# Windowed attention with routed experts on one core: later loads issued in paced pairs behind GpSimd copies, and a new mix of warm-up matmuls

## Chip, cores and metric

The kernel runs on one core of one Trainium2 chip. The metric is the device time of one execution in microseconds. Three executions were timed, and the profile is one further execution.

## What is computed

The reference is an attention with a window of 64 positions over 8 batches, 8 heads, 576 positions and 64 channels, in float32, followed by a mixture of 8 experts with equal capacity.

```python
scores = scale * np.matmul(q, k.transpose(0, 1, 3, 2))
mask = (rel >= 0) & (rel < 64)            # rel = pos[:, None] - pos[None, :]
attn = softmax(np.where(mask, scores, -1e9))
x = np.matmul(attn, v).transpose(0, 2, 1, 3).reshape(4608, 512)
logits = x @ w_gate                        # 8 experts, 576 tokens each
# tokens are given to experts in the order of all logits, best first
out[mask_e] = np.maximum(x[mask_e] @ w1[e], 0) @ w2[e]
```

## The kernel before, in words

The attention is a loop over periods m = 0 to 36 (`for m in range(M + 1)`). A batch has nine blocks of 64 queries, and a period computes two blocks, so a batch lasts four and a half periods. All engines run their instructions in the order in which the loop writes them; there is no reordering, and an engine that waits holds all that stands behind it in its queue.

In period m the loop writes, in this order: the scores of period m in two halves g = 0 and 1 (`qk`: TensorE products of line 128, then on VectorE eight reductions of line 136, four for each half, that add the mask and leave the row extreme in the tile `mx`); the gate products of a new batch (`gate_mm`, line 85, and `gate_cp`); one period after them the gate's turn (`gate_tr`, `gate_out`), which ends with the copies of `even` on GpSimd (lines 114 and 115, two for each of four pairs of blocks, eight in all); the product with the values for period m - 2 (`pv`, line 178); the exponentials of line 141 and the copies of line 153 on ScalarE; then `norm` for period m - 2 on VectorE (`r` in lines 222 and 223, the gate sums, the scaled rows). Into `norm` are woven constants (`more`, two a period, some of them iotas on GpSimd) and a list of small routing steps (`late`, two a period, some of them four comparisons of line 609 on GpSimd). At the end of the period come the stores of finished rows (`store`) and, in the periods named by `loads`, the loads of a later batch (`load_all`), all on the queue of SyncE. For batch 3 and later the gate's turn falls in periods 14, 19, 23, 28 and 32; for batches 1 and 2 the last three pairs of blocks are turned in periods 7 and 12, six copies each.

The tiles of the loop come from the pool `wk`, which gives each name three buffers in turn. `mx` is taken twice a period, once for each half:

```python
wk = ctx.enter_context(tc.tile_pool(name="wk", bufs=3))
mx = wk.tile([128, 4], FT, name="mx")
r = wk.tile([128, 2, 4], FT, name="r")
```

The first line of work in the kernel is a run of matmuls on a tile of zeros (`WARM`, line 49), before the first queries and keys have landed.

After the attention come the routing and the experts (lines 438 to 1377), which the change leaves alone.

Of the kernel before, what the change touches and what calls it, by code (L numbers as in the profile page):

```python
# [20 lines left out]
B, H, S, D = 8, 8, 576, 64  # L21
NB = S // 64
HP = H // 2
E = 8
WARM = 30
VW = 73
DM = H * D
HOLD = 14
LOADED = 9 * (B - 3) + 12


def attention(ctx, tc, c, q, k, v, vt, gate, xs, L, choices, setup, counters, mean, rows, guess):

    nc = tc.nc
# [7 lines left out]
    x = ps.tile([128, 512], FT, name="Tp", bufs=2)  # L42
    SP = [ps.tile([128, 2, 4, 128], FT, name=f"Sp{r}", bufs=1) for r in range(2)]

    z = c["zero"]
    nc.vector.memset(z, 0.0)

    for _ in range(WARM):
        nc.tensor.matmul(x[:, 0:128], z, z, start=True, stop=True)
    masks(tc, c)  # L50
    Q, K, VO, VE, VT = {}, {}, {}, {}, {}

# [35 lines left out]
    def gate_cp(b, i0, i1):  # L88
        nc.scalar.activation(VS[b][:, 64 * i0:64 * i1], VS[b, i0][:, :64 * (i1 - i0)], AF.Copy)
# [27 lines left out]
    def qk(m, g):  # L117

        Sp = [SP[g][:, r] for r in range(2)]
        bi = [divmod(2 * m + a, NB) for a in range(2)]  # L120
        for pp in range(2):
            p = 2 * g + pp
            for a, (b, i) in enumerate(bi):

                k0 = i - 1 if i else 0
                for r in range(2):
                    d = slice(64 * r, 64 * r + 64)
                    nc.tensor.matmul(Sp[r][64 * a:64 * a + 64, pp], Q[b][d, i, p],  # L128
                                     K[b][d, k0:k0 + 2, p], start=True, stop=True)
        kinds = [int(i > 0) for b, i in bi]  # L130
        mk = c["mask"][tuple(kinds)]
        st = wk.tile([128, 4, 128], FT, name="st", bufs=2)
        mx = wk.tile([128, 4], FT, name="mx")
        for h in range(4):

            nc.vector.tensor_tensor_reduce(st[:, h, :], Sp[h % 2][:, h // 2], mk, scale=-0.125, scalar=3.0e38,  # L136
                                           op0=OP.add, op1=OP.min, accum_out=mx[:, h:h + 1])
        pe = wk.tile([128, 4, 128], FT, name="pe", bufs=4)

        def exp(h):  # L140
            nc.scalar.activation(pe[:, h, :], st[:, h, :], AF.Exp, bias=mx[:, h:h + 1], scale=-1.0)  # L141

        return pe, [lambda h=h: exp(h) for h in range(4)]
# [42 lines left out]
    def norm(m, Op):  # L186

        r = wk.tile([128, 2, 4], FT, name="r")
        x = wk.tile([128, H, D], FT, name="x", bufs=HOLD + 4)
        if m % 4 == 0:  # L190
            XL[0] = wk.tile([128, 4, H, E], FT, name="l", bufs=2)
        l = XL[0]

        def scaled():
            for h in range(H):
                nc.scalar.activation(x[:, h], Op[:, h // 4, h % 4, 0:64], AF.Copy, scale=r[:, h // 4, h % 4:h % 4 + 1])
            stores.append((m, x))

        def gates():
            nc.vector.tensor_tensor(l[:, m % 4].rearrange("p (g h) e -> p g h e", g=2), Op[:, :, :, 64:72],  # L200
                                    r[:, :, :, None].to_broadcast([128, 2, 4, E]), OP.mult)
            totals()

        def totals():
            if m in ends:
                j0 = ends[m]
                if m < 32:
                    a = wk.tile([128, 4, 4, E], FT, name="a", bufs=1)
                    nc.gpsimd.tensor_tensor(a, l[:, :, 0:4], l[:, :, 4:8], OP.add)
                    nc.gpsimd.tensor_tensor(a[:, :, 0:2], a[:, :, 0:2], a[:, :, 2:4], OP.add)  # L210
                    nc.gpsimd.tensor_tensor(L[:, j0:m + 1, :], a[:, :, 0], a[:, :, 1], OP.add)
                else:
                    nc.vector.tensor_reduce(L[:, j0:m + 1, :], l[:, j0 % 4:m % 4 + 1].rearrange("p i h e -> p i e h"),
                                            axis=AX.X, op=OP.add)
                late.extend(choices(j0, m + 1))

        def values():
            nc.vector.tensor_tensor(x.rearrange("p (g h) d -> p g h d", g=2), Op[:, :, :, 0:64],
                                    r[:, :, :, None].to_broadcast([128, 2, 4, 64]), OP.mult)
            stores.append((m, x))  # L220

        return [lambda: nc.vector.tensor_scalar(r, Op[:, :, :, 72], 1e-9, None, op0=OP.add),
                lambda: nc.vector.reciprocal(r, r), gates, scaled if m > 32 else values]
# [31 lines left out]
    def load_all(b, part):  # L255
        if not part:
            Q[b] = ld.tile([128, NB, HP, 64], FT, name="Q", bufs=3)
            K[b] = ld.tile([128, NB, HP, 64], FT, name="K", bufs=3)
        else:
            VT[b] = ld.tile([128, NB, HP, 64], FT, name="VT")  # L260
            VO[b] = ld.tile([128, 5, H, VW], FT, name="VO", bufs=3)
        for t, x in ((VT[b], vt), (VO[b][:, 0:4], v)) if part else ((Q[b], q), (K[b], k)):
            t = t.rearrange("p i h w -> p (i h w)").rearrange("p (n x) -> p n x", n=4)
            n = 512 * t.shape[2]
            rows = x[b].rearrange("p x -> (p x)")[0:n].rearrange("(n p x) -> n p x", n=4, p=128)
            for i in range(4):
                nc.sync.dma_start(t[:, i], rows[i])
        if part:
            nc.sync.dma_start(VO[b][0:64, 4].rearrange("p h w -> p (h w)"),
                              v[b].rearrange("p x -> (p x)")[n:n + 64 * H * VW].rearrange("(p x) -> p x", p=64))  # L270

    M = B * NB // 2
    products, turns, loads = {}, {}, {}
# [17 lines left out]
    for m in range(M + 1):  # L291
        exps = [[], []]
        more = [lambda: next(setup, None)] * (0 if not m else 6 if m < 5 else 2)
        if m < M:
            P[m], exps = zip(*[qk(m, g) for g in range(2)])

        for x in products.get(m, []):
            gate_mm(*x)
        old = [x for x in turns.get(m, []) if x not in products.get(m, [])]
        for x in old:  # L300
            gate_tr(*x)
        for x in old:
            gate_out(*x)
        Op = pv(m - 2, T.pop(m - 2), *[last] * (m == M)) if m > 1 else None
        if m == GUESS:
            mean[1](whole[0][:, 0, 5 * VW:5 * VW + 1])
        new = [x for x in products.get(m, []) if x in turns.get(m, [])] if m > 1 else []
        for x in new:
            gate_cp(*x)
            gate_tr(*x)  # L310
            gate_out(*x)
        for f in exps[0]:
            f()
        for x in products.get(m, []):
            if x not in new:
                gate_cp(*x)
        if 0 < m < M:
            T[m - 1], cps = zip(*[tr(pe, m == M - 1 and not g) for g, pe in enumerate(P.pop(m - 1))])
            for n, f in enumerate(exps[1]):
                f()  # L320
                if n % 2:
                    cps[n // 2]()
            if m == 1:
                while more:
                    more.pop()()
                for x in turns[m]:
                    gate_tr(*x)
                    gate_out(*x)
        else:
            for f in exps[1]:  # L330
                f()
        while m == M and late:
            late.pop(0)()
        if m == M:
            for f in reversed(owed):
                f()
        ops = norm(m - 2, Op) if Op is not None else []
        ready = len(late)
        if m == M - 1:
            owed.append(ops.pop())  # L340
        if m == GUESS:
            late.extend(mean[2]())
        for n, f in enumerate(ops):
            f()
            if n > 1 and ready:
                late.pop(0)()
                ready -= 1
            elif more:
                more.pop()()
        for f in more:  # L350
            f()
        if m == GUESS - 1:
            mean[0]()
        for s in (2 * m, 2 * m + 1):
            if stores and (len(stores) > HOLD or s > LOADED):
                store(*stores.pop(0))
        for x in loads.get(m, []):
            load_all(*x)
        if m == PRIME:
            first = wk.tile([8, D], FT, name="first", bufs=1)  # L360
            nc.gpsimd.indirect_dma_start(out=first, out_offset=None, in_=q.rearrange("b p (n d) -> (b p n) d", d=D),
                                         in_offset=IndirectOffsetOnAxis(ap=rows[0:8, 0:1], axis=0))
# [1113 lines left out]
```

## Time and profile before

| what | us |
|---|---|
| median of 3 executions (lowest, highest) | 612.61 (611.14, 616.32) |
| profiled execution, its own time | 613.34 |
| its span in the trace | 611.70 |
| last store of the attention issued at | 150.00 |

The profiled execution is 0.73 us above the median, and its time is 1.64 us more than its span. The attention is the first quarter of the span. Times in the rows are microseconds from the span's start.

### The profile page before, as it was taken

What the parts mean: (1) busy time and instruction counts of PE and PEld (TensorE: products, weight loads), DVE (VectorE), ACT (ScalarE), POOL (GpSimd) and SP (SyncE); (2) the same over time, 40 slices, a digit from 0 to 9 for tenths busy, and PEclk for the clock granted to TensorE, in tenths of its full rate; (3) what the DMA queues carried; (4) which work ended last, traced back from release to release, by engine and by line L of the source; (5) the groups of instructions that cost most, each with busy time, mean ns of one, the idle gap of its engine ahead of it and who ended that gap; (6) DMA issues with size and microseconds to landing.
All of it is one profiled execution on the core that took longest, in us unless ns stands there. A gap on an engine that the chain in (4) does not pass through costs nothing.

```text
span 611.7 us, 15537 instructions
## 1 busy us (share of the span) xinstructions
PE 588.9 (96%) x5713; PEld 503.3 (82%) x5713; DVE 394.1 (64%) x1804; ACT 371.8 (61%) x804; POOL 198.4 (32%) x277
## 2 busy tenths in 40 slices
PE   7899999997699999999999999999999999999995
PEld 6677878886499789878988997898899789889984
DVE  6798988888785587369547936773685466705400
ACT  6799989997465477267537735852774375615410
POOL 1334435862431261054117203511530273011011
PEclk9999999998699999999999999999999999999999
DMA  8999999962698699189748938992895689410001
GB/s 314 362 359 358 362 365 376 384 240 89 183 242 173 247 210 243 43 289 229 152 167 229 245 70 270 216 221 97 257 243 111 233 191 330 169 44 34 2 26 53
DMA packets 46104, 128.87 MB, mean 211 GB/s; under 512 B 5824, under 2 KB 6464, under 8 KB 46016
## 3 DMA queue, kind: packets, MB, share of 16 engines
q1 hardware_dynamic: 31744, 79.00, 36.0%
q0 software_dynamic: 13984, 48.25, 34.1%
q8 instruction: 46, 0.75, 0.5%
q10 hardware_dynamic: 288, 0.52, 0.3%
q14 instruction: 42, 0.34, 0.2%
HBM read 82.14 MB, written 18.87 MB: 165 GB/s over the span
## 4 chain that ended last, share of the span: by engine, by line
PE 50%; issue 15%; DMA 5%; POOL 2%; DVE 1%; ACT 1%; POOLq 0%; SPq 0%
PE h L1328 23%; PE o L1372 20%; PE o L1362 4%; DMA st<-w 2%; DMA wl<-st 2%; POOL out L1351 2%; PE tp L1266 1%; DMA xg<-xs,idx 1%; PE rps L685 1%; PE rps L1046 1%; POOL xg L1228 0%; ACT wh L1155 0%; POOLq L1472 0%; POOL wl L1171 0%; DVE hl L1297 0%
## 5 line engine op out<-in xcount | busy, mean ns | idle before, releaser
L1328 PE MATMUL h<-xh,wh 128*128 128x320 f32 (+2 forms) x800 | 159.0, 333 | 0.3 <-DVE hh L1297 0.3
L1328 PEld LDWEIGHTS h<-xh,wh 128*128 128x128 f32 x800 | 124.2, 188 | 5.6 <-ACT sum L1287 0.5
L1351 POOL DMA_INDIRECT out<-ot,idx x40 | 40.1, 1001 | 198.1 <-DVE q L932 82.1
L1372 PE MATMUL o<-wh,hl 128*128 128x512 f32 x256 | 101.3, 396 | 0.0
L1372 PE MATMUL o<-wl,hh 128*128 128x512 f32 x256 | 100.5, 393 | 0.0
L1372 PE MATMUL o<-wh,hh 128*128 128x512 f32 x256 | 100.4, 392 | 0.0
L141 ACT ACTIVATE pe<-st,mx 128x128 f32<-128x128 f32 x288 | 92.0, 394 | 5.4 <-DVE mx L136 5.0
L1328 PE MATMUL h<-xh,wl 128*128 128x256 f32 (+1 forms) x512 | 91.1, 298 | 0.0
L1328 PEld LDWEIGHTS h<-xh,wl 128*128 128x128 f32 x512 | 78.5, 188 | 4.1
L1171 POOL DMA_DIRECT2D wl<-st x51 | 45.9, 1023 | 82.1 <-ACT wl L1169 43.8
L1155 ACT ACTIVATE wh<-st 128x1024 fp32r<-128x1024 f32 x64 | 67.3, 1051 | 4.9 <-DMA st<-w 4.7
L1342 ACT ACTIVATE ot<-o 128x512 f32<-128x512 f32 x32 | 19.2, 599 | 83.7 <-PE o L1372 83.7
L136 DVE CUSTOM_DVE_ANT_0 st<-Sp,mask 128x128 f32<-128x128 f32 x288 | 63.7, 285 | 5.9 <-PE Sp L128 4.5
L1372 PEld LDWEIGHTS o<-wl,hh 128*128 128x128 f32 x256 | 48.1, 188 | 9.5
L1372 PEld LDWEIGHTS o<-wh,hh 128*128 128x128 f32 x256 | 48.1, 188 | 9.4
L1372 PEld LDWEIGHTS o<-wh,hl 128*128 128x128 f32 x256 | 48.1, 188 | 9.3
L1169 ACT ACTIVATE wl<-wh 128x1024 fp32r<-128x1024 f32 x51 | 53.9, 1058 | 1.0
L1289 DVE TENSOR_TENSOR sum<-h,sum 128x256 f32<-128x256 f32 x56 | 23.4, 418 | 40.3 <-ACT sum L1287 39.7
L1292 ACT ACTIVATE hh<-h 128x320 fp32r<-128x320 f32 (+1 forms) x72 | 30.8, 427 | 30.2 <-PE h L1328 30.0
L1228 POOL DMA_INDIRECT xg<-xs,idx x32 | 32.4, 1012 | 42.2 <-DVE eq L970 34.6
L1297 DVE SCALAR_TENSOR_TENSOR hl<-h,hh 128x256 fp32r<-128x256 f32 x72 | 30.0, 417 | 24.1 <-ACT hh L1292 24.0
L153 ACT ACTIVATE pt<-Tp 128x512 f32<-128x512 f32 x70 | 41.1, 587 | 6.7 <-PE Tp L148 6.6
(222 smaller groups left out, 1028.4 us busy)
## 6 DMA issues: line engine op xcount, KB each, us to landing
st<-w SPq DMA_DIRECT2D x59, 512.0 KB, 7.6
wl<-st POOLq DMA_DIRECT2D x51, 512.0 KB, 8.6
xs<-x SPq DMA_DIRECT2D x36, 256.0 KB, 5.8
VO<-v SPq DMA_DIRECT2D x24, 292.0 KB, 6.4
Q<-q SPq DMA_DIRECT2D x24, 288.0 KB, 6.9
K<-k SPq DMA_DIRECT2D x24, 288.0 KB, 6.2
VT<-vt SPq DMA_DIRECT2D x24, 288.0 KB, 5.8
st<-w POOLq DMA_DIRECT2D x5, 512.0 KB, 7.9
```

Of the source, the lines that this page charges most:

```text
L136: nc.vector.tensor_tensor_reduce(st[:, h, :], Sp[h % 2][:, h // 2], mk, scale=-0.125, scalar=3.0e38, op0=OP.add, op1=OP.min, accum_out=mx[ ...
L141: nc.scalar.activation(pe[:, h, :], st[:, h, :], AF.Exp, bias=mx[:, h:h + 1], scale=-1.0)
L153: return pt, lambda: nc.scalar.activation(flat, Tp, AF.Copy)
L1155: nc.scalar.activation(hi, st[i], AF.Copy)
L1169: nc.scalar.activation(lo, hi.bitcast(FT), AF.Copy, scale=-1.0)
L1171: nc.gpsimd.dma_start(lo.bitcast(FT), st[i], accum_op=OP.add)
L1228: nc.gpsimd.indirect_dma_start(out=g[a][0:n], out_offset=None, in_=self.xs, in_offset=IndirectOffsetOnAxis(ap=idx[0:n, a:a + 1], axis=0))
L1292: nc.scalar.activation(hh[:, f, c0:c1], h, AF.Relu)
L1297: nc.vector.scalar_tensor_tensor(t, h[:, a - c0:b - c0], 0.0, hh[:, f, a:b].bitcast(FT), op0=OP.max, op1=OP.subtract)
L1328: nc.tensor.matmul(h[:, 0:w], wv[:, cc, 128 * (f % 2):128 * (f % 2) + 128], x[:, cc, x0:x0 + w], start=(k == 0), stop=(k == 4 * len(terms) ...
L1351: nc.gpsimd.indirect_dma_start(out=self.out[5 * p + a], out_offset=IndirectOffsetOnAxis(ap=idx[0:m, a:a + 1], axis=0), in_=ot[0:m], in_off ...
L1372: nc.tensor.matmul(o, ht[:, f, 128 * a:128 * a + 128], wt[:, 512 * (f % 2):512 * (f % 2) + 512], start=(k == 0), stop=(k == 23))
```

## The change

The loads of batches 3 to 7 are no longer issued where `load_all` is called. They are put on a list, `pending`, and from period 7 on each period takes up to four of them from it, in two pairs. Ahead of each pair stands a copy of one element on GpSimd into the tile that the pair's first load fills: for the first pair the element is read from `mx` of the period's first half, for the second from `r`. The load has to wait for that copy. The list is filled with 8 loads in periods 7, 11, 16, 20 and 25 and with 9 in the periods after these. The stores stay where they were, each behind a pair. The run of 30 matmuls on zeros with 128 columns becomes 32 of 16 columns followed by 18 of 128.

```diff
-WARM = 30
+WARM, SHORT = 18, 32
+PACED = 7
@@ attention
-    for _ in range(WARM):
-        nc.tensor.matmul(x[:, 0:128], z, z, start=True, stop=True)
+    for n in [16] * SHORT + [128] * WARM:
+        nc.tensor.matmul(x[:, 0:n], z, z[:, 0:n], start=True, stop=True)
@@ qk
+        if not g:
+            seen[0] = mx[0:1, 3:4]
@@ norm
         r = wk.tile([128, 2, 4], FT, name="r")
+        seen[1] = r[0:1, 0, 0:1]
@@ load_all
-            for i in range(4):
-                nc.sync.dma_start(t[:, i], rows[i])
+            pending.extend((t[:, i], rows[i]) for i in range(4))
         if part:
-            nc.sync.dma_start(VO[b][0:64, 4].rearrange("p h w -> p (h w)"), ...)
+            pending.append((VO[b][0:64, 4].rearrange("p h w -> p (h w)"), ...))
+
+    pending, seen = [], {}
+
+    def load(n, after=None):
+
+        for i in range(min(n, len(pending))):
+            t, rows = pending.pop(0)
+            if after is not None and not i:
+                nc.gpsimd.tensor_copy(t[0:1, 0:1], after)
+            nc.sync.dma_start(t, rows)
@@ the loop over m, at the end of a period
+        for x in loads.get(m, []):
+            load_all(*x)
         for s in (2 * m, 2 * m + 1):
+            if m >= PACED:
+                load(2, seen[s % 2])
             if stores and (len(stores) > HOLD or s > LOADED):
                 store(*stores.pop(0))
-        for x in loads.get(m, []):
-            load_all(*x)
+        if m < PACED:
+            load(len(pending))
```

## Rows read from the trace of the kernel before

**Rows 1.** The page, part 1: busy time of each engine, share, instructions.
```profile
PE 588.9 (96%) x5713; PEld 503.3 (82%) x5713; DVE 394.1 (64%) x1804; ACT 371.8 (61%) x804; POOL 198.4 (32%) x277
```
**Rows 2.** Stretches of 10 us: busy time by engine, clock, DMA share, GB/s.
```profile
100.00:110.00 10.00, 10.00 (x234) 8.74 (x229) 9.32 (x64) 10.00 (x32) 9.09 (x18) 1.00 1.01 363
130.00:140.00 10.00, 10.00 (x209) 8.51 (x212) 9.55 (x66) 9.28 (x29) 7.37 (x12) 1.00 0.27 103
```
**Rows 3.** Timeline of DVE: fifth score reduction of periods 8, 13, 15, 20, 24, 26, 29.
```profile
39.27 0.28 DVE L136 CUSTOM_DVE_ANT_0 st<-Sp,mask 128x128 f32<-128x128 f32 x1
...
58.12 0.28 DVE L136 CUSTOM_DVE_ANT_0 st<-Sp,mask 128x128 f32<-128x128 f32 x1
...
66.47 0.28 DVE L136 CUSTOM_DVE_ANT_0 st<-Sp,mask 128x128 f32<-128x128 f32 x1
...
85.00 0.29 DVE L136 CUSTOM_DVE_ANT_0 st<-Sp,mask 128x128 f32<-128x128 f32 x1
...
101.28 0.28 DVE L136 CUSTOM_DVE_ANT_0 st<-Sp,mask 128x128 f32<-128x128 f32 x1
...
107.72 0.28 DVE L136 CUSTOM_DVE_ANT_0 st<-Sp,mask 128x128 f32<-128x128 f32 x1
...
119.60 0.29 DVE L136 CUSTOM_DVE_ANT_0 st<-Sp,mask 128x128 f32<-128x128 f32 x1
```
**Rows 4.** Timeline of GpSimd: its last work of periods 7, 12, 14, 19, 23, 25, 28.
```profile
39.27 0.67 POOL L115 COPY VE<-VO 64x584 f32<-64x584 f32 x1
...
58.23 0.67 POOL L115 COPY VE<-VO 64x584 f32<-64x584 f32 x1
...
68.48 0.67 POOL L115 COPY VE<-VO 64x584 f32<-64x584 f32 x1
...
87.15 0.67 POOL L115 COPY VE<-VO 64x584 f32<-64x584 f32 x1
...
104.93 0.75 POOL L563 IOTA row<- 128x648 bf16 x1
...
107.00 0.25 POOL L211 TENSOR_TENSOR L<-a 128x32 f32<-128x32 f32 x1
107.23 3.97 POOL L609 TENSOR_SCALAR G<-thr,m 128x56 bf16<-128x56 f32 x10
...
122.58 1.59 POOL L609 TENSOR_SCALAR G<-thr,m 128x56 bf16<-128x56 f32 x4
```
**Rows 5.** Timeline of DVE: the first score reduction of period 26.
```profile
106.87 0.29 DVE L136 CUSTOM_DVE_ANT_0 st<-Sp,mask 128x128 f32<-128x128 f32 x1 [0.28 <-ACT pe L141]
```
**Rows 6.** Timeline of ACT in periods 20 and 21.
```profile
84.59 1.86 ACT L141 ACTIVATE pe<-st,mx 128x128 f32<-128x128 f32 x6
...
90.80 0.60 ACT L153 ACTIVATE pt<-Tp 128x512 f32<-128x512 f32 x1 [0.95 <-PE Tp L148]
```
**Rows 7.** Timeline of PE: the dummies, first scores, later scores, a routing sum.
```profile
1.14 3.38 PE L49 MATMUL Tp<-zero 128*128 128x128 bf16 x30 [1.14 <-DVE zero L46]
4.96 1.81 PE L128 MATMUL Sp<-K,Q 64*64 64x128 f32 x32 [0.44 <-DMA Q<-q]
...
48.20 1.10 PE L128 MATMUL Sp<-K,Q 64*64 64x128 f32 x32
...
176.63 0.43 PE L685 MATMUL rps<-G,one 128*128 128x60 bf16 x9
```
**Rows 8.** Timeline of the weight loads: two starts behind "issue".
```profile
18.24 0.14 PEld L85 LDWEIGHTS Tp<-VT,wgs 128*32 128x32 f32 x4 [1.98 <-issue]
...
88.87 0.13 PEld L178 LDWEIGHTS Op<-VE,pt 128*64 128x64 f32 x1 [1.47 <-issue]
```
**Rows 9.** Batch 6: loads issued, gate products; page part 6, us to landing.
```profile
91.88 2.46 SPq L267 DMA_DIRECT2D VT<-vt  x4
...
110.90 0.16 PEld L85 LDWEIGHTS Tp<-VT,wgs 128*32 128x32 f32 x8 [0.42 <-ACT pt L153]
...
VT<-vt SPq DMA_DIRECT2D x24, 288.0 KB, 5.8
```

More of the change, by code (lines that the diff above doesn't have):

```diff
@@ L265, in load_all @@
             rows = x[b].rearrange("p x -> (p x)")[0:n].rearrange("(n p x) -> n p x", n=4, p=128)
-            for i in range(4):
-                nc.sync.dma_start(t[:, i], rows[i])
+            pending.extend((t[:, i], rows[i]) for i in range(4))
         if part:
-            nc.sync.dma_start(VO[b][0:64, 4].rearrange("p h w -> p (h w)"),
-                              v[b].rearrange("p x -> (p x)")[n:n + 64 * H * VW].rearrange("(p x) -> p x", p=64))
+            pending.append((VO[b][0:64, 4].rearrange("p h w -> p (h w)"),
+                            v[b].rearrange("p x -> (p x)")[n:n + 64 * H * VW].rearrange("(p x) -> p x", p=64)))
+    pending, seen = [], {}
[5 more added lines that the diff above has]
+            nc.sync.dma_start(t, rows)
     M = B * NB // 2
```

## The prediction

> **What bounds the kernel now.** I read first the page's busy times [rows 1]: TensorE is busy for 588.9 of 611.7 us, and most of that is the experts, which the change does not touch. So I turn to the attention, the first 150 us, where all the moved work lies. There I read the stretches of 10 us [rows 2]. Between 100 and 110 us TensorE and ScalarE are busy for the whole 10.00 us, VectorE for 9.32 and GpSimd for 9.09, and the DMA engines are full (1.01). Between 130 and 140 us the DMA share is only 0.27, and the three engines that compute are still at 10.00, 9.28 and 9.55. So full DMA queues are not what sets the pace: taking the loads away leaves the period as it is. The pace is a ring of TensorE, VectorE and ScalarE with hardly a gap in it. Two things follow. Thinning the loads has little to give back, and a wait put into VectorE's queue is paid nearly in full, since ScalarE has no reserve with which to catch up.
>
> **The loads themselves.** They are 85 in number and the bytes are the same. Pairs go out in periods 7 to 29, two a period, so 43 copies are added on GpSimd (20 periods with two, 15, 24 and 29 with one). What the thinner queue can give is the sort of stall in which TensorE waits for nothing that the profile shows: 1.98 us at 18.24 and 1.47 us at 88.87 [rows 8]. The first lies ahead of period 7 and stays. The second costs ScalarE 0.95 us in period 21 [rows 6], so I put the gain at 0.95 at most.
>
> **The copy and its place in GpSimd's queue.** A copy of one element is not in the trace. From above it is bounded by a comparison at 3.97 / 10 = 0.40 us, from below by zero; the nearest row is the small sum at 0.25 us [rows 4]. With its hand-over I take 0.2 us. The 43 of them, some 9 us, lie in GpSimd's gaps and cost nothing there. What costs is where they stand: at the end of the period's work on GpSimd, behind the copies of `even`, the iotas and the comparisons.
>
> **The wait that nobody wrote.** The first copy of period m reads `mx` of half 0. That name has three buffers and takes two a period, so the buffer comes round at half 1 of period m + 1: its first reduction, the fifth of that period, may not start before GpSimd has read. Such a wait on a buffer's last reader is in the trace already, for ScalarE's reading: 0.28 us ahead of a first reduction [rows 5]. Behind the waiting reduction VectorE holds three more reductions, `r`, the gate sums and the scaled rows; ScalarE waits for them with the second half's exponentials, and TensorE with the next scores of that half. `r` is taken once a period, so its buffer comes round three periods later, and I cost that wait at nothing. Most periods are safe, since GpSimd is through soon after `r`. Seven are not. For each I set the end of GpSimd's last work ahead of the copy [rows 4] against the start of the fifth reduction one period later [rows 3]:
>
> - period 7, six `even` copies: 39.27 + 0.67 = 39.94 against 39.27, wait 0.67
> - period 12: 58.23 + 0.67 = 58.90 against 58.12, wait 0.78
> - period 14, eight `even` copies: 68.48 + 0.67 = 69.15 against 66.47, wait 2.68
> - period 19: 87.15 + 0.67 = 87.82 against 85.00, wait 2.82
> - period 23, eight copies and two iotas: 104.93 + 0.75 = 105.68 against 101.28, wait 4.40
> - period 25, sums and eight comparisons: 107.23 + 8 x 0.40 = 110.43 against 107.72, wait 2.71
> - period 28, eight copies and four comparisons: 122.58 + 1.59 = 124.17 against 119.60, wait 4.57
>
> That is 18.63 us, and with 7 x 0.2 for the copies 20.0. An earlier wait doesn't shorten a later one, as GpSimd's work in each of these periods starts from VectorE's gate copies or sums of that period and moves along. Periods 26 and 27 come out at about zero by the same sum. Batch 7's turn, in period 32, has no load left and no wait.
>
> **What is absorbed.** ScalarE runs a little behind VectorE: in period 20 its six exponentials take 1.86 us, 0.31 each, so the fifth starts at 84.59 + 1.24 = 85.83, while its reduction ended at 85.29 [rows 3, 6]. That is 0.5 us a wait, 3.5 in all. The 0.95 of period 21 is either relieved or overlapped. 20.0 - 3.5 - 0.95 = 15.6.
>
> **The dummies.** The 30 old ones run from 1.14 to 4.52, 0.11 us apart, and the first scores start at 4.96, when their queries have landed [rows 7]. 18 long ones take 18 x 0.11 = 2.0 us. A short one is bounded above by a long one, 0.11, and below by nothing; the nearest row is a routing sum, nine products of 60 columns with full weights in 0.43 us, 0.05 each with the last one's tail in it [rows 7]. So 32 of them take up to 3.5 us, and the scores start between 0.0 and 1.7 us later (1.14 + 3.5 + 2.0 = 6.6). I take 0.06, near that row: 1.9 us, an end at 5.0 to 5.2 with the last one's tail, and a cost of 0.2. The old dummies leave the first 32 score products at 1.81 us against 1.10 later [rows 7]; that 0.7 us, TensorE's clock not yet risen, can move either way. I take zero.
>
> Each product of that routing sum brings a weight load of its own, so a load and a product together took 0.05 us there. The Trainium skill (TensorE: Matmul & The Clock Gate, section LDWEIGHTS) charges a weight load by its columns, about 107 ns for 128; by that, as an estimate, 32 short dummies would take 3.4 us and the sum would be 1.5 us higher. The trace doesn't agree, and the sum goes by the row.
>
> **Sum.** 15.6 + 0.2 = 15.8, say 16. The profiled execution took 613.34, so 629.3; set against the median, 0.73 lower, 628.6. I predict 629.
>
> **Rival 1, not slower.** The copies reach GpSimd's head before VectorE comes back to the buffer, as they do in 16 of the 23 periods. It takes one thing: that the seven copies don't stand behind the `even` copies and comparisons, or that the buffer isn't reused so soon. The point where it decides is the fifth reduction: a copy done before it costs nothing. Then the time is 613.3 + 0.2 - 0.95, against the median about 612. For it: GpSimd is busy for only 198.4 us of the span [rows 1]. Against it: just in the turn periods it has 5.8 us of work in a row, longer than a period. Chance 0.11.
>
> **Rival 2, faster.** The thinner loads free the whole ring and not only period 21. Against it: the ring is as full with 0.27 of DMA as with 1.01 [rows 2]. Were 3% of the attention's 150 us in the loads, with no wait added, it would be 608 or less with the stall removed. Chance 0.03.
>
> **Rival 3, the loads come late as well.** A blocked copy holds SyncE's queue, stores and all. The value loads of batch 6 go out at 91.88 now; their last piece would go in period 23, behind GpSimd at 105.9, and land 5.8 later at 111.7, against gate products at 110.90 [rows 4, 9]. With no other shift that is 0.8 us late. But under the forecast VectorE's waits up to there (15 us, less what is absorbed) push the products to about 122, so there is margin. It decides if the pieces slip by over 10 us more; with both last batches 5 us late the time is 639. Chance 0.06.
>
> Before the change those loads leave by 94.34 and land by 100.1, 10.8 us ahead of the products; the change gives that margin away. The Trainium skill (DMA: Bandwidth & Descriptors, Rules for kernel authors) says to issue a DMA early and wait for it late, which is the opposite of this change; here the trace has room for the delay, as above.
>
> **How the numbers follow.** The forecast has 0.80. Its own range: with all copies at zero and 1 us absorbed per wait 18.6 - 7 - 0.95 = 10.7, so 623; with 0.4 a copy, nothing absorbed and the dummies' 1.7 it is 18.6 + 2.8 + 1.7 = 23.1, so 636. To hold 8 in 10 I widen it to 617, where only period 14's, 19's or shorter waits come, and to 640 for rival 3. This measurement can tell about 1% (6 us) from no change. Slower by over 1% is forecast and rival 3, 0.86; within 1% is rival 1, 0.11; faster is rival 2, 0.03.
>
> **What would show it.** In the profile of the changed kernel VectorE's line 136 should wait for GpSimd, for some 18 to 20 us in all, in seven waits of which four or five exceed 2 us, all between 39 and 140 us; the one-element copies should stand right behind `even` copies, iotas and comparisons. The stretch from the first scores to the attention's last store should be some 16 us longer, and the experts' stage as long as before. SyncE's queue should wait for GpSimd and the DMA share fall below 1 in the turn periods, with no TensorE wait for Q, K or VT. The prediction is wrong if VectorE shows no wait for GpSimd, if the copies take far longer than 0.4 us, or if the gate products wait for loads.

## The result and the profile after

The changed kernel takes 620.04 us in the median of 5 runs (618.57 to 620.83), the kernel before 611.77 in 5 runs beside it: a ratio of 1.0104, 95% interval 1.0076 to 1.0131. (The ratio is the record's estimate over the executions and not the quotient of the two medians, which are 8.3 us apart.) In a second comparison it was 1.0121 (1.0100 to 1.0142). So it is slower, by 6 to 8 us, where 16 were forecast. The profiled execution took 618.57, its span 616.9. Its last store of the attention is issued at 155.9 (150.0 before), and from there to the end it takes 461.0 us (461.7): in these two profiles the loss is all in the attention, as forecast.

The page of the changed kernel, part 1, answers to [rows 1]: the engines do the same work, and GpSimd has 6.4 us more of it in 43 more instructions.

```profile
PE 590.8 (96%) x5733; PEld 503.9 (82%) x5733; DVE 394.1 (64%) x1804; ACT 372.5 (60%) x804; POOL 204.8 (33%) x320
```

The stretches of [rows 2] in the changed kernel:

```profile
100.00:110.00 10.00, 8.59 (x176) 7.17 (x171) 6.17 (x46) 7.72 (x24) 7.35 (x18) 1.00 0.89 301
130.00:140.00 10.00, 9.46 (x186) 7.05 (x188) 8.72 (x57) 9.04 (x27) 3.83 (x8) 1.00 1.02 369
```

The ring has gaps now: between 100 and 110 us VectorE works for 6.17 us, ScalarE for 7.72. The loads have moved back: the second stretch has a DMA share of 1.02 (0.27 before). What VectorE waits for is told by the view of the score reductions' line (us, times, by who ended the wait; L137 is line 136 of before):

```profile
L137 DVE CUSTOM_DVE_ANT_0 st<-Sp,mask x288: 253/286/293, 6.0 to 147.6; 128x128 f32<-128x128 f32 x144
...
its engine sat idle before it (us, times) until:
  PE Sp L129: 4.5, 12
  POOL VO L282: 3.3, 3
  POOL Q L282: 3.2, 1
  POOL VT L282: 2.2, 1
...
  POOL K L282: 0.4, 1
```

L282 is the one-element copy. The waits on it make 3.3 + 3.2 + 2.2 + 0.4 = 9.1 us in six places. In the timeline (start, duration, what; in brackets the idle time before it and who ended it) the copies stand just where the prediction put them, behind an iota, behind comparisons and behind `even` with comparisons:

```profile
1.14 2.96 PE L50 MATMUL Tp<-zero 128*128 128x16 bf16 x50 [1.14 <-DVE zero L47]
4.84 1.98 PE L129 MATMUL Sp<-K,Q 64*64 64x128 f32 x32 [0.75 <-DMA Q<-q]
...
68.08 0.18 POOL L282 COPY VT<-mx 1x1 f32<-1x1 f32 x1
...
103.82 0.75 POOL L580 IOTA row<- 128x648 bf16 x1
104.52 0.18 POOL L282 COPY VT<-mx 1x1 f32<-1x1 f32 x1
...
104.73 0.29 DVE L137 CUSTOM_DVE_ANT_0 st<-Sp,mask 128x128 f32<-128x128 f32 x1 [2.21 <-POOL VT L282]
...
109.94 1.59 POOL L626 TENSOR_SCALAR G<-thr,m 128x56 bf16<-128x56 f32 x4
111.48 0.17 POOL L282 COPY Q<-mx 1x1 f32<-1x1 f32 x1
...
111.69 0.29 DVE L137 CUSTOM_DVE_ANT_0 st<-Sp,mask 128x128 f32<-128x128 f32 x1 [3.17 <-POOL Q L282]
...
127.55 0.18 POOL L282 COPY VO<-mx 1x1 f32<-1x1 f32 x1
...
127.77 0.29 DVE L137 CUSTOM_DVE_ANT_0 st<-Sp,mask 128x128 f32<-128x128 f32 x1 [2.45 <-POOL VO L282]
```

But most of the reductions that wait are not the ones forecast. 104.73 and 127.77 are the *first* reductions of periods 25 and 30, two periods behind the copies of 23 and 28; only 111.69 is a fifth reduction one period on (period 26). The copy of period 14, at 68.08, which was to cost 2.68 us, costs nothing here (in a second profile of the changed kernel, 0.26).

How the difference grows is read from the starts of `r` on VectorE, one a period. Each column is the kernel's start less that of the kernel before, in us, from one profile each; the last row is the end of the attention. The other kernels come below.

| period | changed | changed, again | six buffers | strict turn | four, strict | early copy | constant | pairs | dummies alone | before, again |
|---|---|---|---|---|---|---|---|---|---|---|
| 2 | +0.07 | +0.13 | +0.04 | +0.16 | -0.01 | +0.27 | +0.03 | +0.32 | +0.14 | -0.54 |
| 3 | -2.04 | -1.98 | -2.06 | -1.95 | -2.12 | -1.84 | -2.08 | -1.79 | -1.97 | -0.24 |
| 8 | -1.16 | -1.31 | -1.48 | -0.66 | -1.76 | -0.66 | -1.48 | -1.61 | -1.33 | -0.24 |
| 14 | -0.66 | -0.14 | +1.85 | +0.92 | -1.13 | -0.52 | -1.05 | +0.66 | -1.19 | -0.24 |
| 15 | -0.53 | -0.12 | +1.78 | +3.86 | -1.24 | -0.65 | -1.19 | +0.53 | -1.31 | -0.25 |
| 20 | -0.53 | +0.07 | +1.70 | +9.13 | -0.73 | -0.64 | -1.02 | +0.99 | -1.29 | -0.29 |
| 24 | -1.11 | -0.54 | +1.68 | +12.14 | -1.31 | -1.57 | -1.65 | +0.07 | -2.22 | -0.73 |
| 25 | +1.10 | +1.66 | +1.93 | +12.45 | +0.89 | -0.08 | -1.49 | +0.07 | -2.22 | -0.73 |
| 26 | +3.98 | +4.52 | +1.82 | +15.32 | +0.53 | -0.47 | -1.57 | +0.07 | -2.22 | -0.54 |
| 30 | +6.32 | +6.82 | +1.78 | +19.94 | +3.07 | +1.03 | -1.67 | +0.05 | -2.24 | -0.52 |
| 37 | +5.88 | +6.36 | +5.06 | +20.15 | +2.95 | +0.54 | -0.97 | +0.04 | -2.23 | -0.52 |

In the changed kernel 2.0 us are gained by period 3, 0.9 of them are lost again by period 24, and the real loss comes in three steps, in periods 25, 26 and 30. The 8.7 us of waits there (2.21 + 3.17 + 0.43 + 2.45 + 0.45) move the end by 5.88 + 1.11 = 7.0.

SyncE's queue does wait for GpSimd, but TensorE has no wait for a later load. The two views of waits, SyncE's and TensorE's (us, times, longest):

```profile
SPq L283 <- POOL VO L282: 16.3, 4, 6.5
...
SPq L283 <- POOL Q L282: 7.6, 2, 4.6
```

```profile
PE Sp L129 <- DVE mx L137: 4.3, 6, 1.8
...
PE Sp L129 <- DMA Q<-q: 0.7, 1, 0.7
```

The one wait for Q is that ahead of the first scores.

### The profile page after: what moved, and what is told of

Its sections match the earlier page's. It is cut to its first block, busy times and chain, and to the rows that moved or that the text cites. A ratio compares the mean times of both kernels' runs of the same rounds, so it can differ in the third digit from the quotient of the medians.

```text
span 616.9 us, 15677 instructions
## 1 busy us (share of the span) xinstructions
PE 590.8 (96%) x5733; PEld 503.9 (82%) x5733; DVE 394.1 (64%) x1804; ACT 372.5 (60%) x804; POOL 204.8 (33%) x320
## 4 chain that ended last, share of the span: by engine, by line
PE 70%; issue 17%; DVE 5%; POOL 5%; ACT 2%; DMA 1%; POOLq 0%; DVEq 0%; ACTq 0%
PE h L1345 25%; PE o L1389 21%; PE Op L181 5%; PE Sp L129 4%; PE o L1379 4%; PE Tp L151 4%; POOL out L1368 2%; DVE st L137 2%; PE tp L1283 1%; PE Tp L86 1%; PE Tp L96 1%; PE rps L702 1%; POOL G L626 1%; PE rps L673 1%; ACT pe L144 1%
## 5 line engine op out<-in xcount | busy, mean ns | idle before, releaser
L1345 PEld LDWEIGHTS h<-xh,wl 128*128 128x128 f32 x512 | 78.5, 188 | 4.0
L137 DVE CUSTOM_DVE_ANT_0 st<-Sp,mask 128x128 f32<-128x128 f32 x288 | 64.0, 285 | 15.0 <-PE Sp L129 4.5
L129 PE MATMUL Sp<-K,Q 64*64 64x128 f32 x1152 | 43.1, 284 | 5.2 <-DVE mx L137 4.3
```

Source lines behind the costliest of these rows:

```text
L1345: nc.tensor.matmul(h[:, 0:w], wv[:, cc, 128 * (f % 2):128 * (f % 2) + 128], x[:, cc, x0:x0 + w], start=(k == 0), stop=(k == 4 * len(terms) ...
```

## The experiments

**Theory A**, formed from this trace: the prediction's wait is real and was priced rightly, but its meeting point was wrong, since `mx` doesn't come round strictly in turn. In the compiled kernel the three buffers, called A, B and C, are handed out like this (period: first half, second half):

```
before:  every period on in turn   0:AB 1:CA 2:BC 3:AB ...
changed: 6:AB 7:CA 8:BA 9:CB 10:AC ... 13:AB 14:CA 15:BA 16:CB ... 22:BC 23:AB 24:CB 25:AC 26:BA ... 28:AC 29:BC 30:AB
```

Period 8's second half is due C, which the copy of period 7 still has to read, and gets A. Likewise C of period 14 comes back in period 16, A of 23 in 25, A of 28 in 30; of the seven, only A of 25 comes back in the next period. **Rivals:** the loss is in the loads (late, or colliding with something), in the copies as such, or GpSimd merely came to the copies at other times than forecast. The kernels below were measured in three sets, each on one chip with the kernel before beside it: its median was 614.82 us beside `strict`, the first `mx6`, `dummies_alone` and `old_dummies`, 612.65 beside the second `mx6`, `const` and the repeats of both kernels, and 613.68 beside the others.

### Strict turn, and more buffers

`strict`:

```diff
-        mx = wk.tile([128, 4], FT, name="mx")
+        mx = wk.tile([128, 4], FT, name=f"mx{(2 * m + g) % 3}", bufs=1)
```

> The changed kernel with mx taken from three names of one buffer each in strict turn, so that every buffer comes round at the next half but two whoever still reads it. Theory A (the prediction's sum was right about the wait and wrong about when the buffer comes round, because the pool doesn't hand the buffers out in strict turn once one has a late reader on GpSimd): VectorE waits for GpSimd in the fifth reductions of periods 8, 13, 15, 20, 24, 26 and 29, 17 to 20 us in all, and the time is 624 to 628. Rival C (the buffer's turn doesn't matter; GpSimd simply reaches the copies sooner than the prediction put them): waits of 9 to 10 us as in the changed kernel and 620.

Measured 633.06 against 614.82, ratio 1.0292 (1.0257 to 1.0327), +18 us. The view of the reductions' line has 7.7 + 7.4 + 3.5 + 0.4 = 19.0 us of waits for the copies. All eight in its timeline, and one wait of TensorE behind them:

```profile
38.61 0.29 DVE L137 CUSTOM_DVE_ANT_0 st<-Sp,mask 128x128 f32<-128x128 f32 x1 [0.86 <-POOL Q L282]
...
60.02 0.29 DVE L137 CUSTOM_DVE_ANT_0 st<-Sp,mask 128x128 f32<-128x128 f32 x1 [0.97 <-POOL Q L282]
...
70.32 0.29 DVE L137 CUSTOM_DVE_ANT_0 st<-Sp,mask 128x128 f32<-128x128 f32 x1 [2.99 <-POOL VT L282]
...
71.31 0.83 PE L129 MATMUL Sp<-K,Q 64*64 64x128 f32 x16 [1.94 <-DVE mx L137]
...
94.13 0.29 DVE L137 CUSTOM_DVE_ANT_0 st<-Sp,mask 128x128 f32<-128x128 f32 x1 [3.07 <-POOL VO L282]
...
113.40 0.29 DVE L137 CUSTOM_DVE_ANT_0 st<-Sp,mask 128x128 f32<-128x128 f32 x1 [4.44 <-POOL VT L282]
...
123.03 0.29 DVE L137 CUSTOM_DVE_ANT_0 st<-Sp,mask 128x128 f32<-128x128 f32 x1 [1.71 <-POOL Q L282]
...
126.41 0.29 DVE L137 CUSTOM_DVE_ANT_0 st<-Sp,mask 128x128 f32<-128x128 f32 x1 [0.43 <-POOL K L282]
...
139.09 0.29 DVE L137 CUSTOM_DVE_ANT_0 st<-Sp,mask 128x128 f32<-128x128 f32 x1 [4.65 <-POOL VO L282]
```

Put beside the prediction's list, with its 0.2 for each copy: 0.87, 0.98, 2.88, 3.02, 4.60, 2.91, 4.77 forecast; 0.86, 0.97, 2.99, 3.07, 4.44, 1.71, 4.65 measured, and 0.43 in period 27. This settles the failed step: with the rotation that the prediction assumed, its waits are there in place and, but for the sixth, in size. The time was above the 624 to 628 expected: the waits were paid in full (in periods 15, 20, 24 and 29 the delay grew by 2.94, 3.13, 4.53 and 4.75 for waits of 2.99, 3.07, 4.44 and 4.65), and they had consequences of their own, below.

`strict4`: the same with `% 4` in place of `% 3`.

> The changed kernel with mx taken from four names of one buffer each in strict turn, so that the buffer of period m's first half comes round at the first half of period m + 2. Theory A, by the prediction's own sum with that meeting point (GpSimd's last work plus 0.2 for the copy, against the first score reduction two periods on, all from the profile of before): period 16: 69.35 against 69.14, 0.2; period 21: 88.02 against 87.66, 0.4; period 25: 105.88 against 103.63, 2.2; period 27: 110.63 against 110.14, 0.5; period 30: 124.37 against 121.99, 2.4; none in periods 9 and 14. That is 5.7 us of waits, between none (six buffers, 1.004) and 9.1 (the changed kernel, 1.012), so 1.008 to 1.010. Rival C (GpSimd reaches the copies at other times than the sum has them): waits of other sizes.

Measured 617.70 against 613.68, 1.0056 (1.0035 to 1.0078). Its timeline:

```profile
68.44 0.29 DVE L137 CUSTOM_DVE_ANT_0 st<-Sp,mask 128x128 f32<-128x128 f32 x1 [0.40 <-POOL VO L282]
...
87.40 0.29 DVE L137 CUSTOM_DVE_ANT_0 st<-Sp,mask 128x128 f32<-128x128 f32 x1 [0.35 <-POOL VO L282]
...
104.52 0.29 DVE L137 CUSTOM_DVE_ANT_0 st<-Sp,mask 128x128 f32<-128x128 f32 x1 [2.21 <-POOL VT L282]
...
111.47 0.29 DVE L137 CUSTOM_DVE_ANT_0 st<-Sp,mask 128x128 f32<-128x128 f32 x1 [1.12 <-POOL Q L282]
...
125.06 0.29 DVE L137 CUSTOM_DVE_ANT_0 st<-Sp,mask 128x128 f32<-128x128 f32 x1 [2.43 <-POOL VO L282]
```

0.2, 0.4, 2.2, 0.5 and 2.4 were forecast for these five, from the profile of before alone; only period 27 is off by more than 0.2, by 0.6. Together they are 6.5 us of waits in the view of the line (5.7 forecast). The time is less than expected (the interval ends at 1.0078).

`mx6`, run twice:

```diff
-        mx = wk.tile([128, 4], FT, name="mx")
+        mx = wk.tile([128, 4], FT, name="mx", bufs=6)
```

> The changed kernel with six buffers for mx in place of three, all else as changed. Theory A (what the change costs is VectorE's wait for GpSimd's read of mx, 9.1 us of waits in the changed kernel's profile): the six waits of over 0.3 us on the line of the score reductions vanish, the attention ends 1 to 2 us before that of the kernel before, since the stalls of 1.98 and 1.47 us that the changed kernel also lost stay lost, and the time is 610 to 611.5. Rival B (the paced loads or the copies themselves cost, through late tiles, SyncE's queue or shared SBUF access): the waits vanish and the time stays at 615 to 620.

> The changed kernel with six mx buffers once more, beside the changed kernel on the same chip. Theory A with E: no wait for GpSimd, 0.6% (4 us) under the changed kernel, and 1.002 to 1.006 of the kernel before, the stalls (before: 43.23, 64.11, 127.17 and 135.87, 5.6 us in all) at other places and of another sum. Rival F: the same four stalls. Rival G (the six buffers only moved the loss, the paced loads cost as much): within 0.2% of the changed kernel.

> The changed kernel once more, unchanged, on the chip of the kernels beside it. All theories: the waits for GpSimd at the same places, 9 us in all, and 1.010 of the kernel before (1.008 to 1.013). Theory E: TensorE's stalls without a releaser differ from those of the first profile (0.70 at 61.67); rival F: the same ones.

In `mx6` no wait for a copy is left. Measured 617.59 against 614.82, 1.0041 (1.0018 to 1.0064); again 615.02 against 612.65, 1.0038 (1.0018 to 1.0059), with the changed kernel at 619.85 beside it. So taking the waits away gives back 619.85 - 615.02 = 4.8 of 7.2 us. For the first run theory A had no loss left at all, and that failed: 2.4 us stay, a third of the loss, and rival B has a part in it. The second run's time is as theory A with E put it, and rival G is out. The repeat of the changed kernel has its waits at the same places, 9.3 us with the 0.26, and its longest stall without a releaser at another place (0.74 at 42.07).

What rival B has is in the two profiles of `mx6`: loads that come late once VectorE no longer waits ahead of them. In the first, VectorE's last gate copies of batches 5 and 7 wait for the values' load:

```profile
100.31 0.22 DVE L105 COPY VO<-Tp 64x64 f32<-64x64 f32 x1 [1.11 <-DMA VO<-v]
...
135.71 0.22 DVE L105 COPY VO<-Tp 64x64 f32<-64x64 f32 x1 [0.93 <-DMA VO<-v]
```

In the second, TensorE waits ahead of batch 7's gate products:

```profile
126.84 0.19 PEld L86 LDWEIGHTS Tp<-VT,wgs 128*32 128x32 f32 x8 [1.83 <-ACT pe L144]
```

The profile puts this one down to ScalarE, but the last load of VT that these products need was issued at 120.19 and took 6.5 us to land, until 126.7. Around it the second run's delay goes from -0.52 us (period 30) to +0.92 (period 31), and around the wait at 100.31 the first run's goes from +0.75 (period 22) to +1.80 (period 23). In the profile of the kernel before neither engine is shown to wait over 0.3 us for a load after the first scores. The two attentions of `mx6` end 5.06 and 1.02 us later than before, so one column of the table says little on what its median keeps.

### The place in GpSimd's queue

`strict_early`, the strict turn of three with the first pair written ahead of its period's `even` copies:

```diff
             P[m], exps = zip(*[qk(m, g) for g in range(2)])
+        for x in loads.get(m, []):
+            load_all(*x)
+        if m >= PACED:
+            load(2, seen[0])
...
-        for x in loads.get(m, []):
-            load_all(*x)
         for s in (2 * m, 2 * m + 1):
-            if m >= PACED:
-                load(2, seen[s % 2])
+            if m >= PACED and s % 2:
+                load(2, seen[1])
```

> The kernel with three mx buffers in strict turn, whose first pair of each period, with its copy of mx, is written right behind the period's scores and so ahead of that period's copies of even on GpSimd (the second pair stays at the end). Theory A (what makes the copy late is that it stands behind the copies of even of its own period): the waits of 18 us shrink to 1 to 4 us, left in periods 25 and 30, where GpSimd is behind by more than a period, and the time is 1.004 to 1.010. Rival H (the reader on GpSimd costs wherever it stands, as by a slow release of the buffer): waits of 10 us or more, 1.015 or more.

Measured 615.18 against 613.68, 1.0024 (1.0006 to 1.0042), less than the 1.004 to 1.010 expected; rival H is out. Of 19.0 us of waits these two are left, in periods 25 and 30 as expected:

```profile
104.39 0.29 DVE L137 CUSTOM_DVE_ANT_0 st<-Sp,mask 128x128 f32<-128x128 f32 x1 [1.38 <-POOL VO L282]
...
123.86 0.29 DVE L137 CUSTOM_DVE_ANT_0 st<-Sp,mask 128x128 f32<-128x128 f32 x1 [1.53 <-POOL VO L282]
```

So the same reader, in the same buffers, makes 16 us less of waits where GpSimd is free to come to it. (The first pair's loads go out earlier too. Of the column's loss by period 4, 1.1 us are TensorE's wait for a load of batch 1 at 21.20, which no experiment touched.)

### What is left without the waits

`const`, the changed kernel whose copies read the constant zeros:

```diff
-                nc.gpsimd.tensor_copy(t[0:1, 0:1], after)
+                nc.gpsimd.tensor_copy(t[0:1, 0:1], z[0:1, 0:1])
```

> The changed kernel with the copies reading the constant zeros in place of mx and r: all 43 copies, the same place in GpSimd's queue, the pairs and the new dummies stay, but no copy waits for the period's sums, and VectorE has no reader on GpSimd to wait for. So loads go out as soon as GpSimd comes to the copy. Theory A: as mx6 or better, 0.998 to 1.004 of the kernel before, no VectorE wait for GpSimd. Rival G (the paced loads, not the reader, carry the loss; here the pairs still stand behind the copies of even on GpSimd): 1.005 to 1.010. If it is below mx6_again by over 0.3%, the waiting of the loads for the sums costs by itself.

`pairs`, without the copies:

```diff
-                load(2, seen[s % 2])
+                load(2)
```

> The changed kernel without the 43 copies: the loads stand in the same pairs at the same places of SyncE's queue, with the stores behind them, and nothing holds them back but that queue. New dummies stay. Theory A (lists and pairs cost nothing by themselves): 0.999 to 1.002, no wait for GpSimd. Rival G (that the later loads collide with other transfers, such as the fetches of TensorE's instructions, costs by itself): as the kernel with copies of a constant or above, 1.0025 to 1.006.

`const` took 614.16 against 612.65, 1.0025 (1.0011 to 1.0039); `pairs` 614.12 against 613.68, 0.9995 (0.9974 to 1.0017). Theory A's forecast holds for both and rival G's for neither. In both, whose copies don't read `mx` or aren't there, the compiled kernel hands the buffers out strictly in turn again. The list, the pairs and the stores between them cost nothing that can be measured. The 43 copies with the holding back of the loads cost some 1.5 us (the intervals of `const` and `pairs`, from two chips, overlap at their ends), and that the loads wait for the sums may add 0.9 more (`mx6` against `const`; the intervals overlap). One place of these 1.5 us shows: in `const` batch 5's last gate copy waits 0.51 us for its load, until 97.01, and the delay goes from -1.95 us (period 22) to -1.50 (period 23); `pairs`, whose loads go out without waiting, has no such wait. How much of the median it explains isn't shown: in the one profile of `const` the attention ends 0.97 us *earlier* than before.

### TensorE's stalls without a releaser

`mx6` has such stalls where its column jumps. From its timeline:

```profile
43.23 0.13 PEld L181 LDWEIGHTS Op<-VO,pt 128*64 128x64 f32 x1 [2.01 <-issue]
...
135.87 0.13 PEld L181 LDWEIGHTS Op<-VE,pt 128*64 128x64 f32 x1 [1.83 <-issue]
```

The DMA queues name a transfer that goes with them. In the stretch 36.1 to 40.6 us of this kernel there are the loads' packets alone; in 40.6 to 40.8 (packets, MB, share of 16 engines) one block of TensorE's instructions is fetched:

```profile
q1 hardware_dynamic: 40, 0.08, 119.4%
q8 instruction: 1, 0.02, 34.8%
```

The fetch begins 2.6 us ahead of the stall's end, and so at 133.3 for that at 135.87. In the kernel before the fetches begin at 15.6 and 86.3, for stalls that end at 18.24 and 88.87 [rows 8]. Counted in the trace, TensorE's instructions up to those two stalls (matmuls, weight loads and the semaphore instructions between them) are 450 and 3,265, 2,815 apart, which is 11 x 256 to within one; in `mx6` they are 1,474 and 5,058, 14 x 256 apart. So TensorE works through blocks of 256 instructions, and each of the eleven such stalls of over 1.3 us in the attentions of this case ends 2.4 to 2.7 us behind the start of a fetch: where the next block's fetch starts later than that ahead of its need, TensorE stands. The Trainium skill (Runtime: NRT & Kernel Launch, section Instruction fetch mechanics) says that an engine's instructions are refilled in blocks of 16 KiB, 256 instructions, and calls crossing a block mostly hidden. The trace agrees on the block; for hidden it has 1.98 and 1.47 us in the kernel before.

`before_again` is the kernel before, unchanged:

> The kernel before once more, unchanged, as a measure of what differs from one execution to the next. Theory E (TensorE's stalls for which the profile names no releaser sit where a block of its instructions ends, and which of these blocks arrives late differs from execution to execution): ratio 1.000, but the stalls over 1 us after period 3 stand at other places than 88.87 us; the one near 18 us comes back, since its fetch started 7.0 us after the block before it was entered and the old dummies set that. Rival F (the stalls belong to the kernel): both stalls at the same places, 1.98 and 1.47 us.

Measured 1.0003 (0.9991 to 1.0014). Both stalls are there again, of other sizes: 2.28 us at 18.01 and 1.05 at 88.14 (for which this profile names a copy of `even` as the releaser), 2.7 and 2.4 us behind fetches that began at 15.3 and 85.7. The second run of `mx6` had one such stall of over 1 us, 1.85 at 42.74, and no other; `pairs` had 2.13 at 43.16. So some places belong to the program and others (135.87 in `mx6`) come and go, and neither theory E nor rival F holds as it was put.

`dummies_alone`, the kernel before with the new dummies, and `mix30`, with 12 short ones and 18 long:

```diff
-    for _ in range(WARM):
-        nc.tensor.matmul(x[:, 0:128], z, z, start=True, stop=True)
+    for n in [16] * 12 + [128] * 18:
+        nc.tensor.matmul(x[:, 0:n], z, z[:, 0:n], start=True, stop=True)
```

> The kernel before with the new dummies (32 of 16 columns, 18 of 128) and the loads as before. Theory A (the new dummies take away TensorE's stall of 1.98 us at 18.24, and what is gained there stays): the period ends come 1.2 to 2 us sooner from period 3 on and the time is 609.8 to 610.7. Rival D (the stall only moves, or what is gained there is lost again at a later wait): 611.5 to 612.5.

> The kernel before with 12 dummies of 16 columns ahead of 18 of 128: as many instructions as before (30), and an earlier end (some 0.7 of 3.4 us less). Theory E (what moves the stall near 18 us is the number of TensorE's instructions ahead of it, so where a block of its instructions ends): the stall is back, 1.5 to 2.5 us at 17.5 to 18.5, with the fetch ahead of it at about 15.5. Rival I (the stall depends on how the dummies fill the time until the first queries): no stall over 0.5 us there. The time is 0.998 to 1.002 of the kernel before in either case.

`mix30` has the stall back, from its timeline:

```profile
18.10 0.14 PEld L85 LDWEIGHTS Tp<-VT,wgs 128*32 128x32 f32 x4 [1.73 <-issue]
```

Its fetch begins at 15.6. All ten profiles with 50 dummies have that fetch at 10.5 to 11.5 and no stall there, all four with 30 have it at 15.3 to 16.4 and the stall: what counts is the number of instructions, not the time that the dummies fill. Yet it is worth nothing measurable: `dummies_alone`, whose profile ends the attention 2.23 us sooner, took 614.81 against 614.82, 1.0002 (0.9981 to 1.0023), as rival D put it, and `mix30` 1.0001 (0.9978 to 1.0025). The profiled execution of `dummies_alone`, at 612.05, was the fastest of its 12. Why the others lose the 2 us again isn't shown.

`old_dummies`, the changed kernel with `WARM, SHORT = 30, 0`:

> The changed kernel with the 30 old dummies. Theory A: TensorE's stall near 18 us is back at about 2 us, the waits for GpSimd stay at 9 us, and the time is 621 to 622. Rival D (the dummies do nothing in the end): 619.5 to 620.5, the stall elsewhere or taken up by the waits.

Measured 623.08 against 614.82, 1.0126 (1.0090 to 1.0162), not to be told from the changed kernel's. The waits are the same, and the stall is back at 19.09, as theory A had it; the time doesn't decide between it and rival D.

No version was faster than the kernel before.

## Why the prediction was wrong in size

- **The ring as the bound: right.** In the strict turn, the four longest waits in VectorE's queue were paid in full.
- **The copy at 0.2 us: right.** 0.17 to 0.18, started 0.12 us apart. That they cost nothing where no reduction waits for them is off by the 1.5 us of `const`, of which only the late load above has a place.
- **The copies' place behind `even`, iotas and comparisons: right**, seen in the timeline, and shown as the cause by `strict_early`.
- **"The buffer comes round at half 1 of period m + 1": the step that failed.** I took "three buffers in turn" literally. The new reader made the pool hand them out in another order, and for the copies of periods 14, 19, 23 and 28 the meeting point came half a period later, by 2.3 to 2.7 us; for 7 and 12 likewise. That turns 2.68 into nothing, 2.82 into 0.35, 4.40 into 2.21 and 4.57 into 2.45; 2.71 of period 25, where the turn was kept, came out at 3.17. So 20.0 us became 9.1. It is what rival 1 named as the point that decides ("or that the buffer isn't reused so soon"), for part of the waits; the sum itself, with the right meeting points, holds to 0.2 us a wait (`strict4`, but for its period 27).
- **Absorbed, 0.5 us a wait:** 7.0 of 8.7 us arrived in the changed kernel, 0.35 a wait absorbed; of the four longest in `strict`, nothing.
- **The stall at 88.87: right**, gone in the changed kernel. **That at 18.24 "stays": wrong**, it went with the 20 more dummies, and the profiled attention gained 2.0 us that the sum didn't have. In the medians this gain doesn't show.
- **The dummies' cost, 0.2: right by luck.** A short one was priced at 0.06 us. The 50 took 2.96 us together, so at 0.11 for a long one a short one took 0.03; they ended at 4.10 and not at 5.0 to 5.2, and the scores started at 4.84 (4.96 before) because their queries landed then. By period 2 the delay is 0.07.
- **Rival 3: not seen in the changed kernel.** SyncE's queue waited for GpSimd, up to 6.5 us at a time, without a late tile, and for the reason that the prediction gave: VectorE's waits push the products back as well. Where those waits are gone (`mx6`, `const`), loads come late, and engines wait 0.5 to 1.8 us for them.

Of the 7.2 us that the changed kernel takes more, then, 4.8 are VectorE's waits for GpSimd's reading; 2.4 are left without them, and of these some 1.5 come with the copies and the loads that they hold back. What the profiles of `mx6` show of them are late loads and fetch stalls, and how the medians divide between the two stays open; that the held-back loads cause the fetch stalls isn't shown, since `pairs` had one too and took no more time than before.

## What to carry to other kernels

Before a slow engine is made to read a small tile, ask which instruction next writes its buffer, and set the reader's end against that start. Take the order of the buffers from the compiled kernel that has the new reader in it, not from the old one's turn: here that halves the sum. A few more buffers for a tile of 16 bytes a partition, or the reader written ahead of the long work in its queue, take most of such a loss away. Then look again at what the waits had hidden: here it was loads with no margin left.

## What was not expected of the hardware

**The clock follows a stall.** In `strict` the granted clock fell to half behind the wait at 70.32. Its stretches 60 to 70 and 71.7 to 78.5 us (us, busy time of TensorE, weight loads, VectorE, ScalarE, GpSimd; clock; DMA share; GB/s):

```profile
60.00:70.00 10.00, 9.37 (x186) 7.63 (x181) 7.18 (x49) 7.25 (x21) 6.72 (x14) 1.00 0.77 252
71.70:78.50 6.80, 6.26 (x84) 5.22 (x76) 4.44 (x32) 4.83 (x15) 0.35 (x2) 0.50 0.98 315
```

TensorE had sat idle for 1.94 us, until 71.31, and then had 1.2 GHz for 6.8 us; in that time the delay against the kernel before grew from 4.09 to 5.94 us, by the starts of `r` in periods 16 and 17 (from a row each that the table leaves out). Two shorter falls followed the waits at 113.40 and 139.09. In the changed kernel a wait left TensorE idle for 1.79 us at 112.68, and between 112.7 and 119.5 us its clock stayed at 1.00; behind the same wait in `old_dummies` (1.78 us, until 116.69) it was at half from 117.3 to 120.8. In `old_dummies` the clock was also 0.50 from 18.4 to 25.2 us, and its `r` of period 3 started 2.72 us later than before. So a wait of 2 us can cost 4; which ones do isn't told by their length alone.

**The instruction fetch** as a stall of 1 to 2 us, which moves with the number of instructions ahead of it, is told above.
